# Pooled attention and a SoLU layer on one core: a new order for all instructions, and score matmuls that alternate between two batches

## The chip, the cores and the metric

One NeuronCore of a Trainium2 chip runs the whole program. The metric is the device time of one execution in microseconds (us). Five in-order engines work side by side: TensorE (PE; its weight loads are listed apart as PEld), VectorE (DVE), ScalarE (ACT), GpSimd (POOL), and SyncE (SP), which here only issues DMAs.

## The reference, cut to what matters

```
k_p, v_p = mean of k, v over groups of 8 rows            # 576 rows become 72
attn = softmax(q @ k_p.T / 8);  x = attn @ v_p           # 8 batches, 8 heads, width 64
h  = x @ w_in                                            # 4608 x 512 @ 512 x 1024
z  = h * softmax(h);  ln = (z - mean) / sqrt(var + 1e-6) * g_ln
out = ln @ w_out                                         # 4608 x 1024 @ 1024 x 512
```

## The kernel before, in words

The 4608 output rows are 36 tiles of 128. Nine tiles serve two batches: four of the first batch, then one **mixed** tile (tiles 4, 13, 22 and 31) whose first 64 rows belong to the first batch and the other 64 to the second, then four of the second.

Every matmul operand is split into two float16 parts, a high one and the rest, so that each product is three float16 products. A tile runs through these steps, each a small function called once per tile:

- `q_hi` (ACT), `q_lo` (DVE for tiles 0 to 3, else POOL): the two parts of q; `q_T`: a DMA transpose.
- `scores` (PE, line 749): 16 matmuls of 72 columns for a plain tile. A mixed tile has 32 of them, because each batch has its own keys; each then fills only 64 columns of the PE array. The result stands in a PSUM buffer of which there is one.
- `s_max`, `s_sub` (DVE), `s_exp` (ACT), `e_sum`, `e_rec`, `e_mul` (DVE): the softmax over 72 keys; `e_hi` (ACT, three pieces), `e_lo` (POOL, two pieces), `e_T` (DMA transpose).
- `av` (PE, line 840): attention times values; `x_hi` (ACT, line 852), `x_lo` (DVE): the two parts of x.
- `mm1` (PE, line 866): x times w_in, three blocks of 8 matmuls of 512 columns; two PSUM buffers.
- `h_max`, `h_nb` (DVE), `h_exp` (ACT), `z_scale`, `z_mul` (DVE), `z_cen`, `z_hi` (ACT), `z_lo` (POOL, in the last tile half on DVE), `z_T` (two DMA transposes), `z_var` (ACT), `n_u` (DVE), `n_f` (POOL): softmax, product and normalization.
- `mm2` (PE, line 990): z times w_out, three blocks of 8 matmuls of 512 columns, into one PSUM buffer named o (tile 34 uses the scores' buffer; tile 35 is done in two halves, the first in o and the second in one of mm1's buffers); `o_evac` (ACT, line 1014) empties it, `o_store` writes it out.

Ahead of the tiles the weights, which arrive as 64-bit floats, are turned into float16 pairs: four pieces of w_in (`wi`) and four of w_out (`wo`), 1 MB each, by `w_load` (DMA), `w_exp` (ACT, line 513), `w_shift` (DVE), `w_abs` (ACT), `w_tail` (DVE, line 541), a maximum over everything (`w_rmax`, `w_par` on PE, `w_all`, `wi_scale`), then `w_hi` (ACT), `w_res` (PE, line 666) with `w_lo` (ACT) for wi, and `w_lo` on DVE for wo. Each batch's q, k and v get a scale from a maximum: `a_max` (DVE), `a_par` (PE), `a_all` and `a_scale` (DVE). k and v are pooled on POOL (`pool_kv`, three levels for each of three parts), v is spread into matmul form by `v_hi`, `v_lo`, `v_put`, and k by `k_hi`, `k_lo`, `k_Td`; for batch 0 k goes through PE instead (`k_two`, `k_T`).

**The order.** All steps are first recorded with `op(...)` as a numbered list of 2253 entries. `ORDER` (line 25), a list of these numbers written out by hand, is then the order in which they are issued. It fixes each engine's own order, since every engine works through its instructions strictly as they were issued, and that of the DMAs on the SP queue. What may run when is left to semaphores: an instruction at the head of its engine waits for its inputs and its buffer, and all behind it wait too.

Of the kernel before, what the change touches and what calls it, by code (L numbers as in the profile page):

```python
# [160 lines left out]
def kernel(  # L161
# [11 lines left out]
    B, H, S, D = q.shape  # L173
# [3 lines left out]
    SP = S // POOL  # L177
# [8 lines left out]
    HB = H // 2  # L186
# [562 lines left out]
    def scores(i):  # L749
        t = tl[i]  # L750
# [680 lines left out]
```

## Time and profile before

| | us |
|---|---|
| median of 3 runs (lowest, highest) | 493.67 (492.72, 494.0) |
| the profiled execution | 493.06 |
| its span, first to last instruction | 491.3 |
| outside the span | 1.76 |
| mean granted TensorE clock | 0.996 |

The profile is of one execution, whose own time is 0.61 us below the median. Times inside it are counted from the start of the span. A busy time includes the pipeline delay of a matmul, so neighbouring matmuls overlap in the listing: eight matmuls of 512 columns are listed with 1.90 us but follow each other after 1.73 us in the chain of waits.

### The profile page before, as it was taken

Reading aid. Unit: us, or ns where it says so; the run is one execution under the profiler, and the core shown is the slowest. Engines: PE = TensorE matmul, PEld = TensorE weight load, DVE = VectorE, ACT = ScalarE, POOL = GpSimd, SP = SyncE. Lnnn points to the kernel's source line nnn. Section 1 sums busy time; section 2 is a strip of 40 time slices with the busy share of each in tenths; the row PEclk is TensorE's granted clock in tenths of the full one; section 3 lists DMA queues with packets and bytes.
Section 4 is the critical chain, followed back from the end, with each engine's and each line's share of the span. In section 5 each row is a group of like instructions: output and inputs, shape, how many; then the busy total and the mean of one; then the engine's idle time right before and its main releaser. Section 6 shows DMA issues by size and latency. Waiting matters only on the chain.

```text
span 491.3 us, 9021 instructions
## 1 busy us (share of the span) xinstructions
PE 448.5 (91%) x3100; PEld 231.6 (47%) x3100; DVE 362.6 (74%) x865; ACT 346.5 (71%) x578; POOL 334.9 (68%) x466
## 2 busy tenths in 40 slices
PE   0137899999999999999999999999999999999996
PEld 0023444445455555555455545554455545545444
DVE  2789999879858886588878967877488886556530
ACT  1678898847896678677875788578676797556742
POOL 4536586798789959984999359967989556361522
PEclk9999999999999999999999999999999999999999
DMA  8998894799977988796899858988987965653443
GB/s 280 384 303 175 216 144 126 156 194 230 221 180 180 209 209 192 168 221 151 190 219 206 179 106 233 182 183 215 215 152 181 178 146 116 106 134 68 94 108 107
DMA packets 201389, 89.14 MB, mean 181 GB/s; under 512 B 177664, under 2 KB 186112, under 8 KB 200832
## 3 DMA queue, kind: packets, MB, share of 16 engines
q1 hardware_dynamic: 201344, 88.57, 78.0%
q8 instruction: 24, 0.39, 0.4%
q14 instruction: 21, 0.17, 0.1%
HBM read 36.70 MB, written 9.44 MB: 94 GB/s over the span
## 4 chain that ended last, share of the span: by engine, by line
PE 79%; DVE 13%; ACT 3%; DMA 3%; issue 1%; SPq 1%; POOL 0%; ACTq 0%; DVEq 0%; POOLq 0%
PE op L1009 34%; PE hp L879 34%; PE xp L847 6%; PE sc L758 3%; DMA wo<-in_moe_w_in_dram 2%; DVE wo L682 1%; DVE wor L549 1%; DVE m L889 1%; DVE z L924 1%; DVE wir L549 1%; PE res_wi L670 1%; DMA eT<-e 1%; DVE q L733 1%; DVE u_wi L528 1%; ACT xT L855 1%
## 5 line engine op out<-in xcount | busy, mean ns | idle before, releaser
L1009 PE MATMUL op<-wo,zT 128*128 128x512 f16 (+1 forms) x888 | 197.4, 373 | 2.4 <-ACT osb L1017 1.8
L879 PE MATMUL hp<-wi,xT 128*128 128x512 f16 x864 | 195.7, 379 | 2.9 <-ACT xT L855 2.4
L879 PEld LDWEIGHTS <-xT 128*128 128x128 f16 x864 | 82.7, 98 | 100.4 <-ACT xT L855 3.7
L1009 PEld LDWEIGHTS <-zT 128*128 128x128 f16 x888 | 84.4, 98 | 93.2 <-DMA zT<-z 2.3
L944 POOL TENSOR_TENSOR z<-z,z 128x512 f16<-128x512 f32 x71 | 83.6, 1187 | 38.7 <-ACT z L938 37.8
L889 DVE TENSOR_REDUCE m<-hp 128x1 f32<-128x1024 f32 x36 | 44.0, 1222 | 39.1 <-PE hp L879 38.8
L826 POOL TENSOR_TENSOR e<-e,e 128x512 f16<-128x512 f32 x36 | 41.8, 1162 | 25.5 <-ACT e L819 25.1
L933 ACT ACTIVATE z<-z,sz 128x1024 f32<-128x1024 f32 x36 | 41.3, 1146 | 24.4 <-DVE z L924 24.0
L330 POOL TENSOR_TENSOR vr<-vr 128x512 f32<-128x512 f32 (+3 forms) x48 | 48.6, 1018 | 9.5 <-DMA vr<-in_v_dram 8.9
L924 DVE SCALAR_TENSOR_TENSOR z<-hp,rs,z 128x1024 f32<-128x1024 f32 x36 | 46.1, 1281 | 5.5 <-ACT z L900 4.0
L900 ACT ACTIVATE z<-hp,nb,Hb 128x1024 f32<-128x1024 f32 x32 | 38.4, 1200 | 16.5 <-DVE nb L892 15.4
L330 POOL TENSOR_TENSOR kr<-kr 128x512 f32<-128x512 f32 (+3 forms) x48 | 42.3, 890 | 6.4 <-DMA kr<-in_k_dram 5.9
L768 DVE TENSOR_REDUCE mx<-sc 128x8 f32<-128x576 f32 x36 | 27.1, 752 | 18.8 <-PE sc L758 18.7
L1017 ACT ACTIVATE osb<-op,f 128x512 f32<-128x512 f32 (+1 forms) x37 | 24.7, 667 | 21.7 <-PE op L1009 8.3
L847 PEld LDWEIGHTS <-vb 128*128 128x128 f16 x640 | 35.1, 98 | 10.2 <-DMA eT<-e 2.0
L847 PE MATMUL xp<-eT,vb 128*128 128x128 f16 (+1 forms) x640 | 38.2, 214 | 0.6 <-DMA eT<-e 0.5
L938 ACT ACTIVATE z<-z 128x1024 f16<-128x1024 f32 x36 | 37.8, 1051 | 0.6
L957 ACT ACTIVATE junk<-z 128x1024 f16<-128x1024 f32 x36 | 37.7, 1047 | 0.2
L782 DVE TENSOR_REDUCE sc<-sc 128x8 f32<-128x576 f32 x36 | 27.4, 762 | 13.0 <-ACT sc L778 13.0
L738 POOL TENSOR_TENSOR q<-qr,q 128x512 f16<-128x512 f32 x28 | 32.5, 1165 | 3.0 <-ACT q L728 2.9
L855 ACT ACTIVATE xT<-xp 128x512 f16<-128x512 f32 x36 | 21.2, 589 | 13.7 <-PE xp L847 13.6
L819 ACT ACTIVATE e<-e 128x512 f16<-128x512 f32 x36 | 22.4, 621 | 10.8 <-DVE e L797 10.6
(230 smaller groups left out, 596.2 us busy)
## 6 DMA issues: line engine op xcount, KB each, us to landing
kr<-in_k_dram SPq DMA_DIRECT2D x16, 512.0 KB, 4.5
qr<-in_q_dram SPq DMA_DIRECT2D x16, 512.0 KB, 4.6
vr<-in_v_dram SPq DMA_DIRECT2D x16, 512.0 KB, 4.7
out_dram<-osb SPq DMA_DIRECT2D x31, 256.0 KB, 3.0
wor<-in_moe_w_out_dram SPq DMA_DIRECT2D x4, 1024.0 KB, 8.4
wo<-in_moe_w_in_dram SPq DMA_DIRECT2D x2, 1024.0 KB, 10.0
wir<-in_moe_w_in_dram SPq DMA_DIRECT2D x2, 1024.0 KB, 11.9
out_dram<-osb SPq DMA_DIRECT2D x10, 128.0 KB, 3.0
```

The costliest lines, as they stand in the source:

```text
L330: nc.gpsimd.tensor_tensor(out=dst, in0=src[:, :, :n], in1=src[:, :, n : 2 * n], op=ALU.add)
L826: nc.gpsimd.tensor_tensor(out=m[:, 1], in0=e_pair(i)[:, :, :P], in1=m[:, 0], op=ALU.subtract)
L847: nc.tensor.matmul(xp[:, c, lo:hi], lhsT=vb[b % 2][:, x, c].rearrange("p j d -> p (j d)"), rhs=eT[:, e, lo:hi], start=(n == 0), stop=(n == 3),
L879: nc.tensor.matmul(hp[:, f], lhsT=xT[:, xt, c], rhs=wi[:, wt, c, f * 512 : (f + 1) * 512], start=(part == 0 and n == 0), stop=(part == 2 a ...
L889: nc.vector.tensor_reduce(out=small(i, "m"), in_=tl[i]["hp"], axis=AX.XY, op=ALU.max)
L900: nc.scalar.activation(z, t["hp"], AF.Exp, bias=t["nb"], scale=hsc(i, 0), accum_out=small(i, "se"))
L924: nc.vector.scalar_tensor_tensor(out=t["z"], in0=t["hp"], scalar=t["rs"], in1=t["z"], op0=ALU.mult, op1=ALU.mult, accum_out=small(i, "sz"),)
L933: nc.scalar.activation(t["zf"], t["zf"], AF.Identity, bias=t["sz"], scale=-float(DFF))
L938: nc.scalar.activation(t["z16"][:, 0], t["zf"], AF.Copy)
L944: eng.tensor_tensor(out=t["z16"][:, 1, fs], in0=t["zf"][:, fs], in1=t["z16"][:, 0, fs], op=ALU.subtract)
L957: nc.scalar.activation(junk, t["zf"], AF.Square, scale=DFF**-0.5, accum_out=small(i, "V"))
L1009: nc.tensor.matmul(op_, lhsT=zT[:, zt, c], rhs=wo[:, wt, c, cols(hf)], start=(part == 0 and n == 0), stop=(part == 2 and n == len(todo) - 1),)
```

## The change

Two things change. `ORDER` is replaced by another permutation of the same 2253 numbers, and `scores` runs over heads and key parts outside and over batches inside, so that in a mixed tile matmuls of the two batches alternate. In a plain tile the loop over batches has one pass, and the 16 matmuls stay in the order they had.

```
 ORDER = (
-    0, 3, 1, 2, 4, 12, 5, 6, 11, 175, 7, 53, 8, 54, 9, 50, 112, 13, 51, 56, 52, 17, 57, 58, 55, 18,
...
-        for b, lo, hi in halves(i):
-            kT = bat[b]["kT"]
-            for h in range(H):
-                o = sc[lo:hi, h // HB, (h % HB) * SP : (h % HB + 1) * SP]
-                for x in range(2):
+        for h in range(H):
+            hc = slice(h * SP, (h + 1) * SP)
+            for x in range(2):
+                for b, lo, hi in halves(i):
                     nc.tensor.matmul(
-                        o, lhsT=t["qT"][:, h, lo:hi], rhs=kT[:, x, h * SP : (h + 1) * SP],
+                        sc[lo:hi, h // HB, (h % HB) * SP : (h % HB + 1) * SP],
+                        lhsT=t["qT"][:, h, lo:hi], rhs=bat[b]["kT"][:, x, hc],
                         start=(x == 0), stop=(x == 1),
                     )
```

Read through the list of steps, the two orders differ by engine as follows (the places that the text below speaks of).

| queue | before | after |
|---|---|---|
| SP, start | kr0, q0, kr1, kr2, q1, g, wi0, wi1, vr2, wi2, wi3, vr0, wo0, q_T(0), vr1 | q0, g, kr0, kr2, kr1, vr2, q1, wi0, wi1, wi2, wi3, wo0, vr0, q_T(0), vr1 |
| DVE, start | a_max(q,0), g_max, shift and tail of wi0, a_max(k), a_max(q,1), a_all(q), small ones mixed with shift and tail of wi1, q_lo(0) | a_max(q,0), g_max, a_max(q,1), a_all(q), three a_scale(q), a_max(k), a_all(k), two a_scale(k), q_lo(0), shift of wi0, ... |
| DVE, up to x_lo(0) | e_mul(2) and a_max(q of batch 1, 0) ahead of x_lo(0), w_tail(wo1) behind | w_tail(wo1) ahead, the other two behind |
| ACT, start | w_exp(wi0), k_two, w_exp(wi1), w_abs(wi0), q_hi(0) | q_hi(0), q_hi(1), k_two, w_exp(wi0), w_exp(wi1) |
| ACT, e_hi of tile 0 | two pieces, then w_abs(wo0), w_exp(wo1), w_lo(wi3), two v_hi, s_exp(1), w_hi(wi2), then the third | three pieces together; w_exp(wo1) behind s_exp(1), w_abs(wo0) behind the third v_hi |
| PE, tiles 4 to 6 | a_par(v of batch 1), mm2(1) last block, scores(4), ..., av(4), scores(6), mm1(4), av(5), scores(8), mm2(3) last block | mm2(1) last block, scores(4), a_par(v of batch 1), ..., mm2(3) last block, av(4), scores(6), mm1(4), av(5), scores(7) |
| PE, tiles 5 to 8 | tile 8 ahead of tile 7 | in the tiles' order |
| PE, end | av(35), mm2(32) three blocks, mm1(35), mm2(34), mm2(33), mm2(35) | av(35), mm2(32) first block, mm1(35), mm2(32) two blocks, mm2(34), mm2(33), mm2(35) |
| ACT, end | h_exp(35), o_evac(34), z_cen(35), z_hi(35), o_evac(33) | h_exp(35), o_evac(32), z_cen(35), z_hi(35), o_evac(34), o_evac(33) |

In all, 241 of 327 PE steps stand at another place, by 2.2 places on average; 717 of 793 on DVE, by 6.5; 422 of 489 on ACT, by 4.0; 336 of 379 on POOL, by 4.2; 214 of 265 DMA steps on SP, by 2.6.

## Rows read from the trace of the kernel before

**Rows 1.** The page, part 1: busy time of each engine, share, instructions.

```profile
PE 448.5 (91%) x3100; PEld 231.6 (47%) x3100; DVE 362.6 (74%) x865; ACT 346.5 (71%) x578; POOL 334.9 (68%) x466
```

**Rows 2.** Stretches: length, busy us by engine, granted PE clock, DMA share, GB/s.

```profile
13.35:52.69 39.34, 18.75 (x99) 8.91 (x100) 35.15 (x69) 30.87 (x47) 18.63 (x22) 0.96 0.98 289
...
48.00:50.00 2.00, 2.00 (x4) 0.81 (x3) 2.00 (x6) 0.92 (x3) 1.99 (x3) 0.50 0.80 230
...
52.00:105.00 53.00, 48.38 (x352) 24.18 (x352) 47.48 (x108) 44.90 (x75) 39.44 (x50) 1.00 0.73 157
105.00:481.00 376.00, 374.95 (x2601) 193.60 (x2600) 277.97 (x680) 267.38 (x452) 269.08 (x372) 1.00 0.78 172
```

**Rows 3.** Chain that ended last, in order of time: start us, us, what.

```profile
4.17 9.16 DMA wo<-in_moe_w_in_dram
13.35 1.13 ACT u_wi L516
...
30.66 0.31 PE g_wi L358
...
52.69 1.90 PE hp L879 x8
54.59 0.52 PE sc L758 x16
...
189.60 1.05 PE sc L758 x32
...
471.41 10.37 PE op L1009 x48
```

**Rows 4.** DVE from 14 to 53.4 us, by shape: count, busy us, mean ns, idle before.

```profile
L733 DVE SCALAR_TENSOR_TENSOR q<-qr,sq('b', 0)_188,q 128x512 f16<-128x512 f32 x4 | 4.0, 994 | 0.0
L349 DVE TENSOR_REDUCE amx_q<-qr 128x1 bf16<-128x1024 f32 x3 | 3.6, 1211 | 0.0
...
L528 DVE TENSOR_SCALAR u_wi<-u_wi 128x1024 int32<-128x1024 int32 x4 | 3.1, 778 | 3.5 <-ACT u_wi L516 3.5
...
L797 DVE TENSOR_TENSOR e<-sc,r 128x576 f32<-128x576 f32 x3 | 2.3, 758 | 0.1
...
L549 DVE SCALAR_TENSOR_TENSOR wor<-wor,u_wo 128x1024 int32<-128x1024 int32 x1 | 1.2, 1215 | 0.0
...
L349 DVE TENSOR_REDUCE amx_k<-kp 128x1 bf16<-128x320 f32 x1 | 0.5, 480 | 0.0
L371 DVE TENSOR_REDUCE pq('b', 0)_187<-gq('b', 0)_183 128x1 f32<-128x256 f32 x1 | 0.4, 425 | 0.4 <-PE gq('b', 0)_183 L358 0.4
```

**Rows 5.** Timeline of ACT, q_hi of tile 0: start us, us, what, idle before it.

```profile
20.63 0.72 ACT L728 ACTIVATE q<-qr,sq('b', 0)_188 128x512 f16<-128x512 f32 x1 [1.91 <-DVE sq('b', 0)_188 L383]
```

**Rows 6.** Timeline of SP: the issue of tile 0's e transpose.

```profile
44.51 1.36 SPq L837 DMA_TRANSPOSE eT<-e  x1
```

**Rows 7.** PE's waits from 52 to 106 us: total us, times, longest.

```profile
PE op L1009 <- ACT osb L1017: 1.0, 1, 1.0
...
PE gv L358 <- DVE amx_v L349: 0.6, 1, 0.6
PE xp L847 <- DMA eT<-e: 0.5, 1, 0.5
```

**Rows 8.** Line 758: stretches of 0.1 us inside a mixed tile's scores, columns as in 2.

```profile
189.83:189.93 0.10, 0.10 (x9) 0.10 (x7) 1.00 1.26 287
189.94:190.04 0.10, 0.10 (x12) 0.10 (x10) 1.00 1.27 289
```

**Rows 9.** Line 758: duration of one matmul, ns, least, median, most.

```profile
L758 PE MATMUL sc<-kT,qT x640: 192/198/268, 30.7 to 443.5; 128*128 128x72 f16 x128, 128*64 128x72 f16 x32
```

**Rows 10.** Timeline of the end: start us, us, what, idle before it.

```profile
482.34 5.32 PEld L1009 LDWEIGHTS <-zT 128*128 128x128 f16 x48 [1.07 <-DMA zT<-z]
...
482.55 5.40 PE L1009 MATMUL op<-wo,zT 128*128 128x256 f16 x48 [0.78 <-ACT osb L1017]
```

**Rows 11.** PE's waits from 106 us on: total us, times, longest.

```profile
PE hp L879 <- ACT xT L855: 0.5, 3, 0.2
```

261 rows, old and new, of the table ORDER are left out of this document.

## The prediction

> **What bounds the kernel now.** I read the page's busy times first: PE works 91% of the span, all others under 75% [rows 1]. A share is an average, so the stretches come next [rows 2]. From 105 to 481 us PE is busy 374.95 of 376.00 us at a granted clock of 1.00: there PE is the bound and only 1.05 us are lost. From 52 to 105 us it idles 53.00 - 48.38 = 4.62 us, while DVE is busy 47.48. From 13.35 to 52.69 us PE has no main work, and DVE is busy 35.15 of 39.34. So a new order can gain in three places: the ramp up to the first block of mm1 at 52.69, the catching-up behind it, and the end. The chain of waits [rows 3] shows the ramp: the first piece of w_in lands at 13.35, its w_exp follows, the maximum over w_in reaches PE at 30.66, the first mm1 starts at 52.69. What starts earlier there is worth its full time, since after 105 us PE merely works off its list.
>
> **Part 1, the ramp.** (a) DVE waits 3.5 us for the first w_exp before its first shift [rows 4]. The new order does q's and k's scales and q_lo(0) ahead of that shift: the second half of q's maximum 1.21, its reduction 0.43, k's maximum 0.48, q_lo 0.99 [rows 4], together 3.1 us that leave the time in which DVE is full. (b) It costs: on ACT q_hi(0), q_hi(1) and k_two stand ahead of the first w_exp. At 0.72 each [rows 5] that is up to 2.2 us by which w_exp starts after the landing at 13.35. On SP, vr2 is now ahead of wi0 and wo0 ahead of vr0; v's pooling may wait for that, but v is wanted after tile 0's softmax. Net of (a) and (b): 0.9 gained. (c) x_lo(0) has e_mul(2) (0.76) and one maximum (1.21) less in front of it and a w_tail (1.22) more [rows 4]: 0.75 gained. (d) tile 0's e transpose was issued at 44.51 [rows 6], held by the third piece of e_hi, behind seven ACT steps. Now the three pieces stand together, so it starts some microseconds earlier, and w_abs(wo0) no longer stands before v_hi. DVE's remaining idle time in the ramp, 39.34 - 35.15 = 4.2 us [rows 2], is what (d) can save at most; some of it is the 1.15 us (13.35 to 14.50) of the first shift's wait, counted in (a). I take half of the other 3.0: 1.6 with rounding. Sum 3.3 us. The bounds: if (a) brings nothing, and (b) costs its 2.2, the ramp is 2.2 longer; if all idle time of DVE goes and (b) costs nothing, 3.1 + 0.75 + 3.0 = 6.9 shorter. One more unknown lies within these: PE's granted clock is 0.50 (the lower of its levels, 1.2 GHz) from 48 to 50 us [rows 2], after a pause of PE; if such a pause falls just before mm1, its first blocks of 1.73 us (10.37 / 6 [rows 3]) take up to twice that. I stay near the middle, because DVE is full on both sides and its work does not shrink.
>
> **Part 2, from 52 to 105 us.** The ramp's gain is handed on, since DVE, the busiest beside PE here, keeps its order up to small swaps. In addition mm2(3)'s last block (1.73 us) now stands before av(4), where PE waited 0.5 for e's transpose, and a_par of v stands behind scores(4), where PE waited 0.6 for it [rows 7]. Both waits have other PE work in front now; behind them the next late thing is the 1.0 us for tile 0's o_evac [rows 7], which has hardly moved. I take -1.0 us; bounds 0 (waits move on) and -4.6 (all idle time).
>
> **Part 3, the mixed tiles.** Their 32 score matmuls take 1.05 us against 0.52 for 16 [rows 3]: 33 ns each in both, though a matmul of a mixed tile fills half the columns. The row that decides is in the middle of such a group, where the first batch ends and the second begins: 12 matmuls are under way there in 0.1 us, against 9 before [rows 8]. With 198 ns for each [rows 9], (100 + 198) / 9 is one each 33 ns, (100 + 198) / 12 one each 25 ns, and that window holds only a piece of the overlap. So the two halves can run at once when their instructions stand close. Alternating all along, 32 should take about 16 x 33 ns = 0.53 us and a little. A few are overlapped already, so I take 0.4 us for each of four tiles: -1.6 us. Bounds: 0, and -2.1 (4 x 0.53). The Trainium skill, TensorEngine Tiling (Array Packing), Key Properties, says that different tiles can load weights and multiply in parallel; by it the sum has its -2.1. Against it stands, in the Trainium skill too, TensorE: Matmul & The Clock Gate, Part 3 (what overlaps and what doesn't): a weight load overlaps running matmuls only when the row group differs, and both batches use all rows; by that the term is 0, the second rival below. The count of 12 speaks for the former page.
>
> **Part 4, the end.** After mm1(35) PE does 10.37 us of mm2 [rows 3], then waits: 0.78 us before the first matmul of tile 35's mm2, 1.07 before its weights [rows 10], for z's transpose and for o. In the new order two blocks of mm2(32) (3.45 us) also follow mm1(35), so tile 35's z has 13.8 us instead of 10.4; z_cen(35) stands before o_evac(34); and mm2(35) begins with the half whose buffer is not o, 0.9 us of work while o_evac(33) runs. The wait goes: -0.9 us; bounds 0 and -1.1. Last in the program are still evacuation and store, so nothing else is late.
>
> **Part 5, the middle.** There is 1.05 us to gain [rows 2]. PE waits there three times for x_hi, 0.2 at most [rows 11], where mm1 follows av with only a scores block between. Counting such places in both lists from tile 4 on: 4, 6, 14, 27 before and 4, 5, 9, 24 after, as many. mm2(7) and mm2(16) follow the tile before them by 0.5 us of other work, so o_evac may cost a few tenths. I take 0; bounds -1.0 and +1.5.
>
> **The sum**: -3.3 - 1.0 - 1.6 - 0.9 = -6.8 us from the profiled execution's 493.06 (span 491.3 and 1.76 around it): 486.3. The median of the runs is 0.61 higher, which gives 486.9, or 487.0.
>
> **Rivals.** (1) The ramp's gain is taken back by tile 4: PE waits there for batch 1's k and v, whose loads queue behind the same weights at a DMA share of 0.98 [rows 2], not for DVE. For it: the wait for e's transpose and amx_v [rows 7]. Against: DVE is full there too. Then half of part 2 and parts 3 and 4 remain: 493.67 - 0.5 - 1.6 - 0.9 = 490.7. Chance 0.20. (2) Alternating brings nothing, as PE's loads for both halves take turns: 487.0 + 1.6 = 488.6. Chance 0.14. (3) The ramp gains its bound of 6.9: 487.0 - 3.6 = 483.4. Chance 0.10. (4) Slower: ACT's new order puts x_hi behind a pass over z (z_cen and its like) in most tiles, and PE, with a block of mm2 too little in front of mm1, waits. At the 0.2 us seen now [rows 11] plus half of q_hi's 0.72 [rows 5], near 0.55 us, 31 tiles cost 17 us; from 12 tiles on the 6.8 us are eaten, and with 25 it is 493.67 - 6.8 + 25 x 0.55 = 500.6. Against it: the counts of part 5. Chance 0.06.
>
> **How the numbers follow.** The forecast has 0.50, its own range 485 to 489.5. About 0.3% (1.5 us) is what a measurement here tells from no change. Faster by more, under 492.2: the forecast, (2), (3) and two thirds of (1), in all 0.86 of 1, less a little for their spread: 0.84. Within 0.3%: the rest of (1) and spread, 0.10. Slower: 0.06. The range leaves out the lower half of (3), (4) and the upper part of (1): 483.5 to 491.5.
>
> **What would show it.** Right: the first mm1 (PE hp L879) near 49.4 instead of 52.69; PE idle from there to 105 us near 3.6; the chain's piece of 32 score matmuls near 0.6 us; no wait before tile 35's mm2; 105 us on as full as now. Wrong: the first mm1 at 52 or later, mixed scores still at 1.05, or PE waits for x_hi or o_evac in many tiles of the middle.

## The result and the profile after

The changed kernel takes 484.62 us (median of 6 runs, 484.57 to 485.67) against 493.07 us (6 runs on the same chip) for the kernel before: ratio 0.9835, 95% interval [0.9817, 0.9853], 8.4 us less. The forecast was 487.0 in a range of 483.5 to 491.5. The sign and the places were right; the ramp gained twice what I gave it, and what lies behind it gained less.

The profiled execution of the changed kernel took 484.65 us with a span of 482.9. The page, part 1, beside [rows 1]: the work is the same, only its share of the shorter span has grown.

```profile
PE 445.8 (92%) x3100; PEld 230.9 (48%) x3100; DVE 362.7 (75%) x865; ACT 345.7 (72%) x578; POOL 335.5 (69%) x466
```

The stretches, beside [rows 2] (length, then busy us of PE, PEld, DVE, ACT and POOL with the number of instructions, granted PE clock, DMA share, GB/s): from 13.35, where the first piece of w_in landed before [rows 3], to the first mm1, from there to mm1 of tile 4, and the middle.

```profile
13.35:45.47 32.12, 17.68 (x99) 9.08 (x98) 30.39 (x64) 28.88 (x44) 15.11 (x18) 1.00 1.08 352
45.47:98.53 53.06, 49.31 (x357) 24.73 (x358) 46.96 (x112) 46.17 (x79) 43.26 (x52) 1.00 0.71 159
105.00:474.00 369.00, 366.59 (x2551) 188.81 (x2548) 276.51 (x673) 265.89 (x448) 265.02 (x366) 1.00 0.81 174
```

The first mm1 starts at 45.47 instead of 52.69 [rows 3] (timeline of PE):

```profile
45.47 3.63 PE L879 MATMUL hp<-wi,xT 128*128 128x512 f16 x16 [0.69 <-ACT xT L855]
```

So **7.22 us** of the gain are there before the first block of the main work. The middle, which was full before (1.05 us idle in 376), is now a little emptier: 369.00 - 366.59 = 2.41 us idle. The chain of waits at three places (start us, us, what): the landing, which comes 1.03 us later; a mixed tile, 1.05 us before; and the end.

```profile
5.20 9.16 DMA wo<-in_moe_w_in_dram
...
182.70 0.64 PE sc L757 x32
...
460.19 19.13 PE op L1009 x112
```

The last row is mm2 of the last three tiles without a break, where the chain before had a stop [rows 3, 10]. PE's waits from 106 to 474 us (total, times, longest), beside [rows 11]: in the middle there are now waits for o_evac, which did not exist there before.

```profile
PE op L1009 <- ACT osb L1017: 1.2, 3, 0.6
PE hp L879 <- ACT xT L855: 0.5, 2, 0.3
PE gq('b', 6)_4590 L358 <- DVE xT L859: 0.4, 1, 0.4
PE xp L847 <- DMA eT<-e: 0.2, 1, 0.2
```

**Where the 8.4 us are.** The last matmul ends at 460.19 + 19.13 = 479.32, before it was 487.96: 8.64 us (0.24 of them are given back by the last store). Stage by stage:

| stage | before | after | difference |
|---|---|---|---|
| start to first mm1 | 52.69 | 45.47 | -7.22 |
| first mm1 to mm1(4); after: without the extra block of mm2(3) (53.06 - 1.73), and with the 0.42 that the mixed tile 4 saves added back | 52.03 | 51.33 + 0.42 | -0.3 |
| four mixed tiles, 1.06 to 0.64 each | | | -1.7 |
| PE's stop before tile 35's mm2 (from the start of the block before it, less 1.73) | 0.94 | 0 | -0.9 |
| middle: PE's waits from 106 us on | 1.0 | 2.3 | +1.3 |

The sum is -8.8; 0.2 us are not assigned.

**The ramp.** A row that is easy to pass over is the duration of single VectorE instructions. Timeline of DVE before (start us, us, instruction): w_tail of the third and fourth piece of w_in and q_lo of tile 2, and below them what POOL did.

```profile
23.20 2.32 DVE L549 SCALAR_TENSOR_TENSOR wir<-wir,u_wi 128x1024 int32<-128x1024 int32 x1
...
27.63 1.21 DVE L549 SCALAR_TENSOR_TENSOR wir<-wir,u_wi 128x1024 int32<-128x1024 int32 x1
...
28.76 1.76 DVE L733 SCALAR_TENSOR_TENSOR q<-qr,sq('b', 0)_188,q 128x512 f16<-128x512 f32 x1
```

```profile
23.17 1.26 POOL L330 TENSOR_TENSOR vr<-vr 128x512 f32<-128x512 f32 x1 [2.92 <-DMA vr<-in_v_dram]
27.98 3.13 POOL L330 TENSOR_TENSOR vr<-vr 128x512 f32<-128x512 f32 x2 [3.54 <-DMA vr<-in_v_dram]
```

The same two views after the change:

```profile
21.83 1.22 DVE L549 SCALAR_TENSOR_TENSOR wir<-wir,u_wi 128x1024 int32<-128x1024 int32 x1
...
29.59 1.12 DVE L733 SCALAR_TENSOR_TENSOR q<-qr,sq('b', 0)_175,q 128x512 f16<-128x512 f32 x1
```

```profile
25.57 2.09 POOL L330 TENSOR_TENSOR vr<-vr 128x512 f32<-128x512 f32 x2 [9.36 <-DMA vr<-in_v_dram]
```

The same w_tail took 2.32 us while POOL pooled v for 1.26, and 1.22 us with POOL silent. The excess of 1.10 is about the part of POOL's instruction that lay ahead of it. In the new order v's first large piece is loaded behind the first piece of w_out, POOL waits 9.36 us for it, and DVE's stretch of w_in work goes by undisturbed. The Trainium skill, SBUF — State Buffer (SBUF: two separate sides), says of the port pair that the two engines share that it is "an **exclusive lock**, not a bandwidth split", against which a DVE instruction with two SBUF inputs blocks; these rows agree (1.22 against 2.32 us). The w_tail at 27.63 fits too: it starts 0.35 us ahead of POOL's instruction at 27.98 and takes 1.21. The DMA engines are as busy beside the fast step as beside the slow one (share 1.03 from 21.83 to 23.05 after, 1.14 from 23.20 to 25.52 before), so it is not the transfers that slow it.

### The profile page after: what moved, and what is told of

Its sections match the earlier page's. It is cut to its first block, busy times and chain, and to the rows that moved or that the text cites. A ratio compares the mean times of both kernels' runs of the same rounds, so it can differ in the third digit from the quotient of the medians.

```text
span 482.9 us, 9035 instructions
## 1 busy us (share of the span) xinstructions
PE 445.8 (92%) x3100; PEld 230.9 (48%) x3100; DVE 362.7 (75%) x865; ACT 345.7 (72%) x578; POOL 335.5 (69%) x466
## 4 chain that ended last, share of the span: by engine, by line
PE 68%; DVE 16%; ACT 6%; DMA 3%; issue 2%; POOL 2%; SPq 1%; ACTq 0%; POOLq 0%
PE hp L879 31%; PE op L1009 29%; PE xp L847 5%; PE sc L757 2%; DMA wo<-in_moe_w_in_dram 2%; DVE m L889 2%; DVE wo L682 1%; DVE z L924 1%; DVE sc L782 1%; DMA eT<-e 1%; DVE sc L771 1%; DVE mx L768 1%; DVE amx_q L349 1%; DVE e L797 1%; DVE wor L549 1%
## 5 line engine op out<-in xcount | busy, mean ns | idle before, releaser
L859 DVE SCALAR_TENSOR_TENSOR xT<-xp,xT 128x512 f16<-128x512 f32 x36 | 24.5, 681 | 10.9 <-ACT xT L855 10.7
```

## The experiments

All ratios are to the kernel before on the same chip. Its median was 492.8 to 493.2 us on the chips used, so medians of runs from two chips can be compared to some 0.3 us only. "New order" is the changed kernel's list, "old order" the one before.

**1. New order, old score loop** and **2. old order, new score loop**: the two halves of the change, each alone.

```
e1   for h: for x: for b, lo, hi in halves(i):      (new)
  -> for b, lo, hi in halves(i): for h: for x:      (as before)
e2   ORDER = the list before;  loop as in the change
```

> The new order with the old scores loop. Theory: each of the four mixed tiles costs PE 1.06 us again instead of 0.64, and PE is the bound, so 4 x 0.42 = 1.7 us come on top: 486.3 us. Rival (the mixed tiles stand where PE has slack): 484.6 us, as with the alternation.

> The old order with the new scores loop. Theory: three mixed tiles save 0.42 us each for certain, the first (at 90 us, ahead of PE's waits) perhaps nothing: 491.4 to 491.8 us. Rival (no gain without the order that was searched for it): 493.1 us.

Measured: the new order alone 486.43 us (485.31 to 492.16, two of eight runs above 491), ratio 0.9897 [0.9863, 0.9931], 1.8 more than the whole change. The new loop alone 492.47, ratio 0.9993 [0.9983, 1.0004]: no difference that can be told. The loop works in both. The chain of waits of the new order with the old loop, at the mixed tile whose row in the changed kernel is 0.64:

```profile
183.58 1.05 PE sc L757 x32
```

Not all of the 1.8 is the alternation. The last matmul of this trace ends 1.70 us later than in the changed kernel. 0.50 of that comes from the ramp, whose last part ran at a granted clock of 0.59 here and at 1.00 there, and is still there at mm1(4). The four mixed tiles add 4 x 0.42 = 1.68, but the wait for o_evac(28) at mm2(29) is 0.38 shorter than in the changed kernel (0.23 against 0.61). So in the traces the alternation brings 1.7 us, of which the next wait takes back 0.4.

In the old order the mixed scores also last 0.64 us, but PE then stands until o is empty (timeline of PE in the second kernel):

```profile
189.60 0.71 PE L756 MATMUL sc<-kT,qT 128*64 128x72 f16 x32
190.55 1.67 PE L1008 MATMUL op<-wo,zT 128*128 128x512 f16 x7 [0.24 <-ACT osb L1016]
```

Before, the block of mm2 began 1.06 us behind the tile's first score matmul (189.53 to 190.59), here 0.95 us (189.60 to 190.55). Over the four mixed tiles the old order keeps 0.15, 0.11, 0.15 and 0.42 us, 0.83 of 1.68. What follows: alternating saves 0.42 us a tile, and it is worth that only where the next block does not wait for a buffer that is emptied at its own time. In the new order what stands there (a_par of v, av, or an mm2 whose buffer is free) does not wait in any of the four. The two halves of the change need each other for about half of these 1.7 us.

**3. New order only up to the first mm1** and **4. new order only from there**: is the gain of the ramp kept?

```
e3   ORDER = new up to mm1(0), first block;  old behind it;  old loop
e4   ORDER = old up to mm1(0), first block;  new behind it;  old loop
```

> The new order up to the first block of mm1, then the old order for all that is left; old scores loop. Theory: the first mm1 starts 7.2 us earlier, as in the changed kernel, and this is handed on to the end: 493.1 - 7.2 = 485.9 us. Rival (tiles 1 to 4 wait for batch 1's preparation, whose place in the order is the old one): the lead is gone by mm1 of tile 4, 490 to 493 us.

> The old order up to the first block of mm1, then the new order for all that is left; old scores loop. Theory: only the stretch behind the ramp (-0.2), the middle (+1.4) and the end (-0.9) differ: 493.3 us, as before. Rival (the new order's gain lies in all of its length): 487 to 490 us.

Measured: 490.34 us, ratio 0.9949 [0.9933, 0.9966], and 492.43 (491.13 to 497.25), ratio 1.0013 [0.9988, 1.0039]. In the first the ramp's gain is complete and then lost again; timeline of PE:

```profile
45.33 1.90 PE L878 MATMUL hp<-wi,xT 128*128 128x512 f16 x8 [0.69 <-ACT xT L854]
48.85 0.68 PE L757 MATMUL sc<-kT,qT 128*128 128x72 f16 x16 [1.62 <-DVE e L796]
...
50.49 0.28 PE L357 MATMUL gq('b', 1)_524<-identb,amx_q 128*128 128x128 bf16 x1 [0.90 <-DVE amx_q L348]
50.57 5.29 PE L878 MATMUL hp<-wi,xT 128*128 128x512 f16 x16
```

PE runs ahead of DVE, waits 1.62 and 0.90 us for it, and its 16 matmuls then take 5.29 instead of 3.63 us, at a granted clock of 0.51 from 50.5 to 54 us. In the changed kernel the second block of mm1(0) stands ahead of scores(3) and fills that time. At mm1(4) 3.3 us of the lead are left, at the end 2.5. So of 7.2 us only about 2.5 stay if nothing behind the ramp is arranged for it. In the fourth kernel's trace (its profiled execution took 491.13 us, the fastest of its runs) the stop before tile 35's mm2 is gone (112 matmuls in 19.28 us, as in the changed kernel), and the middle waits 1.9 us instead of 1.0. The new order from tile 0 on is worth next to nothing without the new ramp: it is there to keep the ramp's gain.

**5. q's and k's scales first, in the old order**: step (a) of the prediction alone.

```
 DVE:  + a_max(q,1), a_all(q), three a_scale(q), a_max(k), a_all(k), two a_scale(k), q_lo(0)
         ahead of the first w_shift
 ACT:  + q_hi(0), q_hi(1) behind the first w_exp
```

> The old order; only q's and k's scales and q_lo(0) stand ahead of the first w_shift on VectorE, and q_hi(0), q_hi(1) right behind the first w_exp on ScalarE. Theory (the ramp is VectorE's work, and its waiting for the weights is what the new order fills): the maximum over w_in reaches PE some 2 to 3 us earlier than 30.66, and the first mm1 starts as much earlier than 52.69; of that, mm1 of tile 4 keeps 1 to 2 us: 491 to 492 us. Rival (the ramp is bound by the weights' arrival and ScalarE's passes): the first mm1 stays at 52 to 53.

Measured: 493.19 us, ratio 1.0003 [0.9992, 1.0014]: nothing. The timeline of DVE shows why:

```profile
16.97 1.76 DVE L528 TENSOR_SCALAR u_wi<-u_wi 128x1024 int32<-128x1024 int32 x1
18.76 1.63 DVE L549 SCALAR_TENSOR_TENSOR wo<-wo,u_wi 128x1024 int32<-128x1024 int32 x1
...
23.33 2.18 DVE L549 SCALAR_TENSOR_TENSOR wir<-wir,u_wi 128x1024 int32<-128x1024 int32 x1
...
27.63 2.27 DVE L549 SCALAR_TENSOR_TENSOR wir<-wir,u_wi 128x1024 int32<-128x1024 int32 x1
```

The 3.49 us that the first shift waited are filled, as forecast, but now four weight steps lie beside POOL's pooling of v and take 3.5 us more than the 0.69 and 1.22 they take alone. The last of them is the step that took 1.21 before. It starts at 27.63 there too, but here POOL is 0.07 us ahead of it and not 0.35 behind (timeline of POOL), and it takes 2.27: who starts first decides.

```profile
27.56 2.93 POOL L330 TENSOR_TENSOR vr<-vr 128x512 f32<-128x512 f32 x2 [3.12 <-DMA vr<-in_v_dram]
```

The first mm1 starts at 53.21, later and not earlier.

**6. New order, but v's first piece loaded early again**: the opposite test, whether POOL's silence is worth anything in the new order.

```
 SP:   wi3, wo0, vr0      ->      wi3, vr0, wo0
```

> The changed kernel with one swap on the SP queue: the load of v's first part stands before the first piece of w_out again, as in the old order. Theory (pooling v on GpSimd while VectorE converts the weights is what slowed single VectorE instructions from 1.2 to 2.3 us before): slow w_tail instructions are back, the maximum over w_in reaches PE about 1 us later than 25.87, and of this up to 1 us is left at the end: 484.6 to 485.6 us. Rival (the slow ones were by chance, or v's later arrival costs): the same time or less, 483.6 to 484.6.

Measured: 486.53 us, ratio 0.987 [0.9854, 0.9886], 1.9 more than the changed kernel. Timeline of DVE, then of POOL:

```profile
24.09 1.14 DVE L528 TENSOR_SCALAR u_wi<-u_wi 128x1024 int32<-128x1024 int32 x1
25.26 1.63 DVE L549 SCALAR_TENSOR_TENSOR wir<-wir,u_wi 128x1024 int32<-128x1024 int32 x1
...
28.49 1.54 DVE L528 TENSOR_SCALAR u_wo<-u_wo 128x1024 int32<-128x1024 int32 x1
```

```profile
23.41 2.40 POOL L330 TENSOR_TENSOR vr<-vr 128x512 f32<-128x512 f32 x2 [7.05 <-DMA vr<-in_v_dram]
```

These three steps took 0.68, 1.23 and 0.87 us in the changed kernel: 1.5 us more, and DVE comes to them 0.4 later (w_tail at 22.22 instead of 21.83). Together that is the 1.90 us by which the first mm1 is late (47.37). Nearly all of it is left at the end, more than the expectation gave it. So the place of one 512 KB load decides whether DVE's work on w_in is slowed.

**7. New order, ten steps of ACT as before** (pieces of e_hi of tile 0, w_abs(wo0), w_exp(wo1) and v_hi in the old sequence): step (d) alone undone.

```
 ACT:  e_hi(0) x3 together  ->  two pieces, w_abs(wo0), w_exp(wo1), w_lo(wi3), v_hi, s_exp(1), w_hi(wi2), third piece
```

> The changed kernel; ten ScalarE steps from e_hi of tile 0 to v_hi stand in the old order again (two pieces of e_hi, w_abs, w_exp, w_lo, two v_hi, s_exp, w_hi, then the third piece). Theory (VectorE's work sets the pace, PE's first blocks only follow): tile 0's transpose and the first mm1 start 2 to 4 us later than 45.47, but only 0 to 1 us of it is left at the end: 484.6 to 485.6. Rival (av of tile 0 is the ramp's bound, and what it loses stays lost): 486.6 to 488.6 us.

Measured: 486.16 us, ratio 0.9857 [0.9838, 0.9876]; the first mm1 at 46.56. Step (d) is worth 1.1 us in the ramp, and mm1(4) keeps 1.0 of it: less than the theory's 2 to 4 us, but it stays, which the theory denied. Tile 0's e transpose is issued at 39.69 in this kernel, at 35.55 in the changed one and at 44.51 before [rows 6], but in none of the three does PE wait for it: av(0) follows w_res without a stop. The way is another one. v_hi stands behind w_abs and w_exp again, and DVE waits for it ahead of v_lo (timeline of DVE):

```profile
37.78 1.68 DVE L469 SCALAR_TENSOR_TENSOR v<-vp,sv,v 128x256 f16<-128x256 f32 x1 [0.74 <-ACT v L451]
```

In the changed kernel that v_lo takes 1.52 us and DVE does not wait for it. With it e_mul(1) is late, and scores(2), which needs its buffer, starts at 41.98 instead of 40.90: there the whole 1.1 us is already lost.

**8. New ramp and end around the old middle**: does the new middle cost anything by itself?

```
 ORDER = new up to av(5);  old up to av(35);  new behind it;  new loop
```

> The new order up to av of tile 5, then the old order up to av of tile 35, then the new one; with the alternation. Theory (the middle of the new order loses 1.4 us more than that of the old one): 484.6 - 1.4 = 483.2 us, faster than both. Rival (what PE waits for in the middle is not of the order, but comes and goes with the transfers): 484.6 us or more, with waits at other tiles.

Measured: 491.48 us, ratio 0.9969 [0.9955, 0.9984]. The splice made a wait of its own (PE, timeline):

```profile
109.76 1.14 PE L757 MATMUL sc<-kT,qT 128*128 128x72 f16 x16 [4.83 <-DMA qT<-q]
```

The old list takes tile 8 ahead of tile 7, the new one does not, so a transpose of q was issued too late. That wait and the granted clock behind it (0.54 from 110 to 116 us) account for the loss. The run says little about the middle, only how tightly such a list is tied. The second run, the old order with the new loop, says more: from 111 to 480 us PE idles 1.18 us there, against 2.24 from 111 to 474 in the changed kernel.

```profile
111.00:480.00 369.00, 367.82 (x2564) 189.63 (x2562) 272.29 (x672) 265.39 (x448) 263.37 (x364) 1.00 0.78 172
```

```profile
111.00:474.00 363.00, 360.76 (x2505) 185.72 (x2504) 270.84 (x659) 262.56 (x443) 259.10 (x360) 1.00 0.81 173
```

So the new middle waits about 1 us more than the old one, in one trace of each.

**9. Old order with the fifth run's edit and the new start of SP and POOL**: if contention was what ate step (a), loading v late must give it back.

```
 as 5, and:  SP's first 15 loads and POOL's first 18 steps as in the new order
```

> The old order with q's and k's scales and q_lo(0) ahead of the first w_shift, as in the run before of that kind, and in addition the first 15 loads on SP and GpSimd's first 18 pooling steps (batch 0's k and v) in the new order, so that v's large parts come after the first piece of w_out. Theory (VectorE gains only where GpSimd is silent meanwhile): w_tail back at 1.2 us, the maximum over w_in reaches PE at about 26 to 27 instead of 30.66, the first mm1 2 to 3 us before 52.69; as the old order behind it keeps its own slow VectorE steps, 1 to 3 us are left: 490 to 492 us. Rival (the loads' order does not matter on the old order): 493 us, as without it.

Measured: 491.79 us, ratio 0.9977 [0.9967, 0.9987], 1.1 less than before; the first mm1 at 50.78. Timeline of DVE, the step that is 2.32 us long in the kernel before and 2.18 in the fifth run, and the end of w_in's maximum:

```profile
22.22 1.23 DVE L549 SCALAR_TENSOR_TENSOR wir<-wir,u_wi 128x1024 int32<-128x1024 int32 x1
...
29.17 0.15 DVE L557 TENSOR_REDUCE g_wi<-bnd_wi 128x1 bf16<-128x4 f32 x1
```

In the fifth run that last step is at 30.95. The first piece lands 2.0 us later here than there (15.14 against 13.12), probably because v's third part (vr2) is now loaded ahead of it, and yet the maximum is done 1.8 us earlier: undisturbed weight steps and the filled wait give 3.8 us, the landing takes 2.0. The 26 to 27 us of the theory are missed, since the old order has q_lo(2) between the last w_tail (done at 26.77) and the maximum, and it waits 1.27 us for ScalarE.

**10. New order, batches alternating in pairs** (for h, for b, for x: two matmuls of one batch, two of the other).

```
 for h:  - for x:  for b:     + for b:  for x:
```

> The changed kernel, but in mixed tiles the batches alternate after every two matmuls (both key parts of a head) and not after each. Theory (PE lets the two halves of its columns run beside each other as far ahead as the instructions stand in its queue, as at the border between the batches before): nearly all of the overlap stays, 0.6 to 0.75 us per mixed tile, 484.6 to 485.0 us. Rival (only direct neighbours overlap): half of the gain or less, 0.85 to 1.06 us per mixed tile, 485.5 to 486.3 us.

Measured: 485.06 us, ratio 0.9847 [0.9834, 0.986]. The chain's row of a mixed tile:

```profile
183.10 0.66 PE sc L757 x32
```

In the timeline the next block begins 183.69 - 183.05 = 0.64 us behind the first score matmul, as in the changed kernel (183.27 - 182.63). The median is 0.4 us higher because the list is 0.42 late already at this tile (183.05 against 182.63), from the ramp, and stays so; the scores have no part in it. The halves of the array work side by side when two instructions of one half follow each other, too.

**11. New order with four moves to fill the middle's waits.**

```
 PE:   mm1(17) third block behind mm2(15) third block;  mm1(24) first block behind mm2(22) first block
       a_par(q of batch 6) behind mm1(24) second block
 ACT:  o_evac(28) ahead of q_hi(34), q_hi(35)
```

> The changed kernel with four steps moved where PE waits in the middle: mm1(17)'s last block behind mm2(15)'s last, mm1(24)'s first behind mm2(22)'s first, a_par of batch 6's q behind mm1(24)'s second block, and on ScalarE o_evac(28) ahead of two q_hi. Theory (from tile 5 on PE is the bound, so each wait is worth its length): waits of 0.41, 0.49, 0.55 and 0.77 us go, 2.2 us in all, 482.4 us. Rival (they turn up again as other waits, since what PE waits for is late anyway): 484 to 485 us.

Measured: 490.94 us, ratio 0.9963 [0.9951, 0.9975]: 6.3 us slower than the changed kernel. PE's timeline and DVE's at the place:

```profile
258.32 0.23 PE L358 MATMUL gk<-identb,amx_k 128*128 128x128 bf16 x1 [2.90 <-DVE amx_k L349]
```

```profile
255.46 1.22 DVE L889 TENSOR_REDUCE m<-hp 128x1 f32<-128x1024 f32 x1 [10.57 <-PE hp L879]
...
257.77 0.49 DVE L349 TENSOR_REDUCE amx_k<-kp 128x1 bf16<-128x320 f32 x1
```

I moved a block of mm1 on PE and left the maximum that reads it where it stood on DVE. DVE, in order, stood 10.57 us before it, with k's maximum behind it, for which PE waited 2.90; from 260 to 264 us the granted clock was 0.72. In 240 to 280 us PE is busy 35.84 of 40.00, after the change 39.75. A step moved on one engine must be moved on the engines that read it. The move of o_evac did what it should: PE has no wait from 400 us on.

**12. New order with the move of o_evac(28) alone.**

```
 ACT:  o_evac(28) ahead of q_hi(34), q_hi(35)
```

> The changed kernel with one ScalarE step moved: the eviction of tile 28's output (o_evac(28)) ahead of the two q passes of tiles 34 and 35 in ScalarE's list, nothing else. In the changed kernel's trace the output projection that wants this PSUM buffer waits 0.6 us at 410.80 (0.77 with the gap around it), the largest wait after tile 4. Theory (from there TensorE is the bound, so a wait taken away stays away): the wait at 410.8 is gone, no new wait over 0.3 us stands behind it, and the last output matmul starts 0.5 to 0.8 us earlier: 483.8 to 484.1. Rival (the list is so tightly tied that the time turns up in the next wait, as in the mended kernel): TensorE waits about as long a little later, 484.4 to 484.8.

Measured: 484.47 us (483.97 to 485.12, 5 runs), ratio 0.9826 [0.9813, 0.984]. The row that it removes, from PE's timeline of the changed kernel:

```profile
410.80 3.40 PE L1009 MATMUL op<-wo,zT 128*128 128x512 f16 x15 [0.61 <-ACT osb L1017]
```

PE's wait is gone, and two stops of 0.13 and 0.23 us before and behind a score block 3 us later take a part of its place. From the mm1 block near 105 us to the last stretch of mm2 PE needs 0.45 us less (105.24 to 459.34, against 105.47 to 460.02). The theory holds in the trace at the lower edge of its size; the medians, 0.15 us apart, cannot tell the two kernels apart.

## Why the prediction was partly right

**Part 1, the ramp: right place, half the size.** I took 3.3 us, it was 7.22, above even my bound of 6.9. Three things were wrong.

(1) How full DVE is. I wrote that "DVE is full on both sides and its work does not shrink" and therefore stayed near the middle of my bounds. It was not full, and its work shrinks a little. From the start of the span to scores(2), the last time that PE waits for DVE's e_mul before mm1, DVE does the same list but for one half of v_lo (0.34) and one shift of w_out (0.69), which come later in the new order. The stretches:

```profile
0.00:45.74 45.74, 31.32 (x68) 1.00 0.94 296
```

```profile
0.00:40.90 40.90, 29.71 (x67) 1.00 1.01 326
```

Of the 4.84 us, 45.74 - 31.32 - (40.90 - 29.71) = 3.23 are idle time and 1.61 are less DVE work. Most of the idle time, 2.5 us, went from ahead of the first shift, which is step (a). Of the work, 1.0 is only put off. The rest is less interference from POOL: w_tail -1.10, q_lo -0.64, two shifts of w_in -0.26 and -0.11, against +1.04 on a v_lo (0.48 to 1.52) that now meets POOL and +0.19 on a shift of w_out, together -0.9 (neighbouring instructions overlap by some hundredths, so the parts add up to a little more than the whole). The trace of before had shown it: the 1.76 and 2.32 us stand beside 0.73 and 1.22 for the same shape in the same list. I read means of shapes [rows 4] and not single rows.

(2) Steps (a) and (b). (a) was right as a mechanism and wrong as a price: alone it is worth nothing (run 5), because the weight steps that move forward fall onto POOL; with v loaded late (run 9) it brings 1.3 us net to the maximum, 3.1 less a landing that comes 1.8 later. (b) was a misreading on my side: the list of steps gives w_exp(wi0) as ACT's first step in both orders; the table before the prediction and the prediction put q_hi and k_two ahead of it. The cost of up to 2.2 us does not exist. What does exist there is the landing, which I named on SP but gave no price: +1.03 us for the first piece. Of the loads ahead of it only vr2 is new, so that is the likely cause; no run moves vr2 alone. With 1.03 in place of 2.2 the term would have been some 1.2 us larger.

(c) was 0.75 and is nothing at the first mm1: from av(0) to it both traces have 1.74 us (50.95 to 52.69, 43.73 to 45.47). The first block of mm1(0) reads x_hi alone; x_lo is wanted by the second. (d) was 1.6 and is 1.1 (run 7), by way of v_hi and not of e's transpose, which PE never waited for there.

(3) What I had only as an unknown: from scores(2) to the first mm1 it is 6.95 us before and 4.57 after. The clock suggests itself, since from 46.99 to 50.95 it was granted at 0.57 before. The runs say otherwise: in the old order with full clock (runs 2, 4 and 9) the same stretch is 6.31 us each time, so the clock costs only 0.64. The other 1.74 are PE's waits for two steps of ACT: 0.7 for a w_lo of w_in, which empties the buffer that w_res(wi2) needs, and 1.0 for x_hi(0). Timeline of ACT in the fourth run, full clock, old order:

```profile
50.09 1.05 ACT L538 ACTIVATE ab_wo<-u_wo 128x1024 bf16<-128x1024 f32 x1
51.04 0.19 ACT L538 ACTIVATION_READ_ACCUMULATOR ab_wo<-u_wo 128x1 f32 x1
51.13 0.59 ACT L854 ACTIVATE xT<-xp 128x512 f16<-128x512 f32 x1
```

PE waits 1.69 us there for x_hi, behind a w_abs of w_out (wo2); in the new order that w_abs stands behind x_hi(0), and PE waits 0.69. At low clock the wait for x_hi was hidden behind slow matmuls, so one trace could not show both. The clock itself is not the order's doing: the first run, with the new order, had low clock in this stretch and took 6.21 us for it. The ramp's sum is 4.84 + 1.74 + 0.64 = 7.22.

**Part 2, 52 to 105 us: the gain is handed on, its own term is small.** -1.0 forecast, -0.3 measured. The waits moved on, as in my lower bound. Both waits of [rows 7] named there, e's transpose and v's maximum, are gone, but from the first mm1 to mm1(4) PE still waits 1.1 for o_evac, 0.6 for z's transpose and 0.9 for x_hi of tile 1. The first rival (the ramp's gain taken back by tile 4, 490.7) did not come. Run 3, a list that is not changed behind the ramp, ends near its number (490.34), but by another wait than the rival's: PE waits for DVE's e_mul and maximum of q, not for the loads of k and v.

**Part 3, the mixed tiles: right.** -1.6 forecast, -1.7 measured by the rows; run 1's 1.8 holds 0.5 of a lower clock in the ramp, and 0.4 of the 1.7 came back as a longer wait for o_evac(28). The count of 12 matmuls in 0.1 us [rows 8] was the row that decided. Of the two pages I set against each other, TensorEngine Tiling (Array Packing) of the Trainium skill is borne out (0.64 us for 32, against 0.52 for 16 that fill the array); the rule in TensorE: Matmul & The Clock Gate, Part 3, that a weight load overlaps only with another row group would have left 1.05. The second rival (488.6) is out. What I missed: half of the gain needs an order in which what follows the mixed tile does not wait (run 2).

**Part 4, the end: right.** -0.9 forecast; the stop of 0.94 us is gone.

**Part 5, the middle: 0 forecast, +1.3 measured**, inside its bounds (+1.5). "mm2(7) and mm2(16) follow the tile before them by 0.5 us of other work, so o_evac may cost a few tenths" was the sentence that held, for two of the three waits for o_evac: 0.31 us at mm2(7) and 0.25 at mm2(16). I had that price and left it at 0. The third and longest, 0.61 at mm2(29), I had not seen: o_evac(28) stands behind two q_hi there (run 12). Run 8, meant to price the new middle by itself, tested its own splice instead; by the trace of run 2 the new middle waits about 1 us more than the old one. The fourth rival (x_hi behind passes over z, 500.6) is out: x_hi costs 0.5 us there, as before.

The third rival, the ramp at its bound of 6.9 us and 483.4, was the nearest to what happened in the ramp, for another reason than I gave it. That the total came near is in part luck, since errors of opposite sign met: the ramp was 3.9 us better and parts 2 and 5 together 2.0 worse than forecast. The 0.61 us that I added for the median did not come, since here the profiled execution (484.65) is as long as the median. Two small slips stand in the prediction's sums: half of 3.0 is 1.5 and not 1.6, and the chances counted as faster add up to 0.87 and not 0.86. Neither bears on the above.

## What to carry to other kernels

Before an engine is called full, look at the single durations of its costliest shapes: where one shape takes 1.2 us here and 2.3 there, the engine is being slowed, and the time of a load can be worth more than the order of the steps. A gain in a ramp is kept only if the engine that then runs ahead has its own work in front of the next wait; priced without that, most of it is lost. In a list that fixes every engine's order a step can't be moved on one engine alone, since what reads it stands in another queue.

## What the runs showed of the hardware

- GpSimd work on SBUF slows single VectorE instructions by 1 us and more: w_tail 2.32 against 1.22 us, and a plain shift with one input 1.76 against 0.69 (run 5). A w_tail that starts 0.35 us ahead of GpSimd's instruction keeps its 1.21 us; one that starts 0.07 behind it takes 2.27 (run 5). Four kernels with the load of v at different places agree (runs 5, 6 and 9, and the changed kernel).
- 32 score matmuls over halves of the array's columns take 0.64 us if the halves alternate, one by one or two by two, and 1.06 if 16 of one half come first. Each time is from the first score matmul to the next instruction of other work.
- After the wait of 0.97 us before scores(2) PE's granted clock was 0.59 from there to av(0) in run 1 and 1.00 in the changed kernel, with the same order on PE (0.50 is the lower of its levels). Where another engine is late behind it, that costs 0.64 us (6.95 - 6.31, the old order), else 1.64 (6.21 - 4.57).
